# Attention: where a unit's output transposes stand, which engine inverts its sums, and one written order for each kind of two steps

## The chip, the cores and the metric

The kernel runs on one core of a Trainium2 chip. The metric is the device time in microseconds (us) of one execution; the time before is the median of three runs. The engines are TensorE (PE; its weight loads are shown apart as PEld), VectorE (DVE), ScalarE (ACT), GpSimd (POOL) and SyncE (SP, which only issues DMAs here).

## The reference, cut to what matters

One transformer block on 2048 rows of 576 columns, all in float32. The change lies in the attention.

```python
h = _layernorm(x) * (1 + ca) + sa
qkv = (h @ wqkv) -> q, k, v                     # 32 heads of 18 columns
scores = einsum("bhqd,bhkd->bhqk", q, k) * 18 ** -0.5
p = softmax(scores)                             # over 2048 keys
o = einsum("bhqk,bhkd->bhqd", p, v)
x = x + ga * (o.reshape(B, S, D) @ wo)
h = _layernorm(x) * (1 + cb) + sb
x = x + gb * ((sigmoid(h @ w_gate) * (h @ w_up)) @ w_down)
```

## The kernel before

The program has four stages: projections of q, k and v; the attention loop; the gated feed-forward part on the first 1024 rows; the same on the last 1024 rows. Only the attention loop is changed.

**Units, steps, periods.** A unit is two heads on one half of the query rows (1024 rows); there are 32 units (`u`), the number of pairs of heads (16) times two halves. A unit has 16 steps (`kt`), one for each 128 keys. The loop handles two steps at a time, an even one and the odd one after it; such two steps are called a period here, so a unit has eight periods, named by their even step: kt 0, 2, 4 to 14.

**What a step puts on PE.** Four score tiles (`t`, line 1055): 128 keys by 512 queries, for head h = 0 or 1 and column half c = 0 or 1; ACT turns each into exponentials (line 1059). Four maxima tiles (`m`, line 524): queries by 512 keys of a later unit, 22 steps ahead; DVE reduces each to row maxima (line 530). Of the eight maxima tiles of a period, one (head 0, keys 0, called `r` below) is copied by ACT with a Relu (line 533), and another (head 0, keys 1, called `x`) is joined with that copy by one DVE instruction (line 535). Head 0 lies in rows 0 to 63 of the PE array and head 1 in rows 64 to 127, so a tile of head 0 and one of head 1 that follow each other in the program run side by side: they are called a pair. Every tile takes the next of seven PSUM banks in turn (`bank()`), so a tile can be written only when the tile seven places before it has been read by ACT or DVE. The exponentials of a step are multiplied with v by `values()` (line 629): four column groups of the array at once, all 512 queries (`V`, `v` in the old strings) or 256 of them (the half runs `A` and `B`, `a` and `b`).

**Orders.** PE and ACT follow the order in which the code is written (a manual schedule); DVE, POOL and SP are ordered by the scheduler. The order of a step is a string, one letter for each action. Where a background step of TensorE is due (`state["next"] == "g"`), a period takes the order "full", otherwise "halved". In a halved period the even step runs the values of the step two before (`v`), then the first half of the last step's (`a`); the odd step runs the second half (`b`):

```python
order = ("vmmtmmtsactt", "wmcmbkttmtmt") if halved else ("vtmmttmvtm", "ktmwttmctmm")
```

The letters: `k` calls `taken()`, in which ACT copies the finished sums of a unit from PSUM to SBUF (`oT`, line 646). `w` or `s` starts what is due: at kt 3 `outputs()`, whose first part is four 128x128 transposes of `oT` into one bank (line 656); when a unit's maxima are complete `spread()`, one transpose (line 555); and one step of the background work (`rows0`, `rows1`: the projection with wo and the second layer norm of finished rows, whose PE parts are lines 743, 760, 776 and 886). `c` runs the second parts: for `outputs()` the reciprocal of the softmax sums on DVE, read from PSUM (line 661), ACT's copy of the bank (line 672), and two POOL multiplications into the rows of outputs (line 676). In the halved order `w` is the first thing of the odd step, so that the four transposes stand between a pair of score tiles and a pair of maxima tiles, after half run A and ahead of half run B. `SIDES`, `SIDES_H`, `MAXIMA` and `MAXIMA_H` say which head and column half each `t` and `m` takes.

**POOL's other work in the loop** is splitting and scaling `w_down` (units 4 to 14) and, from unit 15 on, the float32 splits of the background work that TensorE uses one or two periods later (lines 750, 751, 762 to 764, 866).

Of the kernel before, what the change touches and what calls it, by code (L numbers as in the profile page):

```python
# [15 lines left out]
F32 = mybir.dt.float32  # L16
F32R = mybir.dt.float32r
AF = mybir.ActivationFunctionType
ALU = mybir.AluOpType
# [4 lines left out]
P = 128  # L24
S = 2048
# [3 lines left out]
DH = 18  # L29
# [10 lines left out]
LEAD = 6  # L40
FROM0, FROM1 = 15 * 16, 27 * 16 + 8
# [6 lines left out]

MAXIMA = ((1, 0), (0, 0), (1, 1), (0, 2), (1, 2), (0, 3), (0, 1), (1, 3))
SINGLE = (0, 1)  # L50
MAXIMA_H = ((1, 0), (0, 0), (1, 1), (0, 2), (0, 3), (1, 2), (0, 1), (1, 3))
SIDES_H = ((1, 0), (1, 1), (0, 1), (0, 0))
SIDES = ((0, 0), (0, 1), (1, 0), (1, 1))
ORDERED = 7
SEVENS = NB - 2
TURNS = {1: 1, 6: 2, 2: 4, 7: 3, 5: 5, 4: 7, 3: 6}
ROWS_FROM = 1
SECOND = 7 * NB


@with_exitstack
def tile_block(ctx, tc, x_in, wqkv, wo, w_gate, w_up, w_down, c_in, w_mod, out):
    nc = tc.nc
# [10 lines left out]
    make_identity(nc, ident)  # L74
    powers = const.tile([P, 8], F32, name="powers")
    nc.gpsimd.memset(powers, -0.5)
    mcol = const.tile([P, 2, 5], F32, name="mcol")
    mcol2 = const.tile([P, 2, 6], F32, name="mcol2")
    gb_b = const.tile([P, D], F32, name="gb_b")
# [420 lines left out]
    def maxima():  # L500


        n = HW // P
        last = None
        for u in range(UNITS):
            qs, ks = heads(u)
            mx = mxs[u % 2]
            if u not in SINGLE and u - 2 in SINGLE:
                nc.gpsimd.memset(mx[:, 0:n, 1], LOWEST)
            for i in range(8 * n):  # L510
                if last is not None and i == (9 if u == 1 else 8):
                    if u == 1:
                        for _ in spread(*last):
                            pass
                    else:
                        state["spread"] = last
                qt = i // 8
                pairs = u not in SINGLE
                h, kc = (MAXIMA_H if state.get("halved") else MAXIMA)[i % 8]
                rows = slice(64 * h, 64 * h + 3 * DH)  # L520
                paired = pairs and h == 0 and kc < 2
                at = NCH if paired and kc == 0 else kc
                sp = bank()
                nc.tensor.matmul(  # L524
                    sp, qs[rows, qt * P : (qt + 1) * P],
                    ks[rows, at * 512 : (at + 1) * 512], start=True, stop=True,
                )
                to = mx[:, h * n + qt, kc : kc + 1]
                if not paired:
                    nc.vector.tensor_reduce(to, sp, axis=AX.X, op=ALU.max)  # L530
# [38 lines left out]
    todo = maxima()  # L569
    state = {}  # L570

    def turn():
        if turns["s"] < turns["to"]:
            turns["s"] += 1
            next(todo, None)

    def run():
# [71 lines left out]
    def outputs():  # L649
# [11 lines left out]
        nc.vector.reciprocal(rec, tq[:, :, :, DH])  # L661
        if half == 1 and p == H // 2 - 1:
            state["last"] = epool.tile([P, 512], F32, name="oT")[:, 0 : 16 * DH].rearrange("p (t e) -> p t e", t=8)
            for h in range(2):
                nc.vector.tensor_tensor(
                    state["last"][:, :, h * DH : (h + 1) * DH].rearrange("p (c b) e -> p c b e", c=2),
                    tq[:, 2 * h : 2 * h + 2, :, 0:DH],
                    rec[:, 2 * h : 2 * h + 2, :].unsqueeze(3).to_broadcast([P, 2, 4, DH]),
                    op=ALU.mult,
                )  # L670
            return
        nc.scalar.copy(oT, tp.rearrange("p b q -> p (b q)"))
        tq = oT.rearrange("p (b j e) -> p j b e", j=4, e=32)
        for h in range(2):
            f0 = (2 * p + h) * DH
            nc.gpsimd.tensor_tensor(
                Os[half][:, :, f0 : f0 + DH].rearrange("p (c b) e -> p c b e", c=2),
                tq[:, 2 * h : 2 * h + 2, :, 0:DH],
                rec[:, 2 * h : 2 * h + 2, :].unsqueeze(3).to_broadcast([P, 2, 4, DH]),
                op=ALU.mult,  # L680
            )
# [328 lines left out]
    for u in range(UNITS):  # L1010
# [5 lines left out]
            Os.append(big.tile([P, 8, 640], F32, name="big"))  # L1016
        for kt in range(NT):
            step = u * NT + kt
            turns["to"] = 64 + 4 * LEAD + 4 * (step + 1)
            kcols = slice(kt * P, (kt + 1) * P)  # L1020
            if kt % 2 == 0:
                heavy = state.get("next") == "g"
                hold = heavy and (kt == 2 or kt == 12 and u < UNITS - 1)
                state["halved"] = step >= 10 and (hold or not heavy)
            halved = state["halved"]
            sides = iter(SIDES_H if halved else SIDES)
            probs = [None] * 4
            order = ("vmmtmmtsactt", "wmcmbkttmtmt") if halved else ("vtmmttmvtm", "ktmwttmctmm")
            for does in order[kt % 2]:
                if does == "m":  # L1030
                    turn()
                elif does == "k":
                    taken()
                elif does in "ws":
                    if kt == 3:
                        follow.append(outputs())
                        next(follow[-1], None)
                    if "spread" in state and halved == (does == "s"):
                        follow.append(spread(*state.pop("spread")))
                        next(follow[-1])  # L1040
                    if step >= FROM0 and not hold and halved == (does == "s"):
                        state["next"] = next(rows0 if step < FROM1 else rows1, None)
                elif does == "c":
                    while follow:
                        next(follow.pop(0), None)
                elif does == "v":
                    if step >= LAG:
                        values()
                elif does in "ab":
                    values(slice(0, 256) if does == "a" else slice(256, 512))  # L1050
                else:
                    c, h = next(sides)
                    sT = bank()
                    rows = slice(64 * h, 64 * h + 3 * DH + 2)
                    nc.tensor.matmul(  # L1055
# [733 lines left out]
```

## Time and profile before

| | us |
|---|---|
| median of 3 runs | 2802.2 (2801.63 to 2802.61) |
| span of the profiled execution | 2801.3 |
| PE busy in it | 2766.6 (99%) |
| DVE busy | 2302.7 (82%) |
| ACT busy | 1607.0 (57%) |
| POOL busy | 816.2 (29%) |

The profiled execution is known by its span, from the first to the last instruction; the median of the runs is 0.9 us above it. Sums are made against the span and then shifted by these 0.9 us. The attention loop's values run from 238 us to 1534 us. PE's busy time counts modelled ends of overlapping matmuls; where PE loses time is therefore read from the starts of its rows in the timeline, not from its busy share.

### The profile page before, as it was taken

To read this page: it belongs to the slowest core of one execution; us is meant where nothing else is said; L and a number is where in the kernel's file an instruction comes from. 1 tells how busy PE (TensorE), PEld (TensorE's weight loads), DVE (VectorE), ACT (ScalarE), POOL (GpSimd) and SP (SyncE) were. 2 spreads that over 40 slices of the span, in tenths; PEclk is the share of its full clock that TensorE was granted. 3 is DMA by queue.
4 is the path that set the end of the run, shared out by engine and by line. 5 is a ranking of instruction groups with operands and counts; after the bars stand their busy time and mean duration, and the time that the engine had idled before them with its cause. 6 is when DMAs were issued, how large, how long until landed. Compare 5 with 4: busy or idle time off the path is not lost.

```text
span 2801.3 us, 50850 instructions
## 1 busy us (share of the span) xinstructions
PE 2766.6 (99%) x18637; PEld 1830.4 (65%) x18637; DVE 2302.7 (82%) x4370; ACT 1607.0 (57%) x3051; POOL 816.2 (29%) x1077
## 2 busy tenths in 40 slices
PE   7999999999999999999999999999999999999999
PEld 5975444444444444444444888888888888888888
DVE  7278999999998888999883788888898677777777
ACT  3216999999999778999888322333333222222221
POOL 3125208887843111663113222222221100000000
PEclk9999999999999999999999999999999999999999
DMA  5344215444442120232126766667767966666663
GB/s 173 123 155 147 72 59 173 168 173 157 170 135 80 36 59 24 98 106 71 43 68 219 266 220 228 232 217 266 279 249 274 355 201 196 203 196 200 199 197 120
DMA packets 170778, 462.60 MB, mean 165 GB/s; under 512 B 21212, under 2 KB 88032, under 8 KB 160416
## 3 DMA queue, kind: packets, MB, share of 16 engines
q1 hardware_dynamic: 150064, 360.72, 38.7%
q0 software_dynamic: 20464, 98.62, 10.0%
q8 instruction: 147, 2.41, 0.4%
q14 instruction: 103, 0.84, 0.1%
HBM read 281.92 MB, written 176.82 MB: 164 GB/s over the span
## 4 chain that ended last, share of the span: by engine, by line
PE 93%; DVE 4%; issue 1%; DMA 1%; ACT 1%; POOL 0%; SPq 0%; DVEq 0%; ACTq 0%; POOLq 0%
PE x L1196 28%; PE o L629 19%; PE s L1055 12%; PE s L524 10%; PE d L1346 8%; PE d L1278 6%; PE s L310 4%; PE s L776 2%; PE s L363 1%; DVE mx L530 1%; PE s L656 1%; ACT p L1059 1%; DMA wq_raw<-in_A_wqkv_dram 0%; DVE Oa L1350 0%; DVE w L1186 0%
## 5 line engine op out<-in xcount | busy, mean ns | idle before, releaser
L1059 ACT ACTIVATE p<-s 128x512 f32<-128x512 f32 x2048 | 1078.1, 621 | 98.8 <-PE s L1055 83.5
L530 DVE TENSOR_REDUCE mx<-s 128x1 f32<-128x512 f32 x1568 | 993.8, 683 | 108.0 <-PE s L524 93.3
L629 PE MATMUL o<-p,vaug 128*32 128x256 f32 (+1 forms) x5848 | 592.4, 477 | 3.1 <-ACT p L1059 2.5
L1055 PE MATMUL s<-q,k 56*128 56x512 f32 x1920 | 516.6, 449 | 0.0
L524 PE MATMUL s<-k,q 54*128 54x512 f32 x1920 | 501.3, 427 | 2.6 <-DVE t L746 1.7
L524 PEld LDWEIGHTS s<-k,q 54*128 54x128 f32 x1920 | 275.6, 185 | 231.6 <-DVE mx L535 161.0
L1055 PEld LDWEIGHTS s<-q,k 56*128 56x128 f32 x1920 | 246.9, 184 | 242.7 <-issue 112.8
L1196 PE MATMUL x<-k,w 128*128 128x512 f32 x1512 | 368.6, 391 | 0.0
L1196 PEld LDWEIGHTS x<-k,w 128*128 128x128 f32 x1512 | 276.9, 188 | 53.1 <-issue 1.7
L629 PEld LDWEIGHTS o<-p,vaug 128*32 128x32 f32 x5848 | 115.4, 108 | 209.7 <-issue 130.7
L1346 PE MATMUL d<-wd,hh 128*128 128x288 f32 x1248 | 249.9, 295 | 2.4 <-DVE Oa L1350 2.4
L1196 PE MATMUL x<-big,w 128*128 128x512 f32 x1008 | 244.9, 391 | 2.1 <-DVE u L1690 1.4
L1196 PE MATMUL x<-w,w 128*128 128x512 f32 x1008 | 245.1, 391 | 0.0
L1196 PEld LDWEIGHTS x<-big,w 128*128 128x128 f32 x1008 | 185.1, 188 | 38.5 <-DVE u L1690 2.3
L1196 PEld LDWEIGHTS x<-w,w 128*128 128x128 f32 x1008 | 184.4, 188 | 34.3
L1346 PEld LDWEIGHTS d<-wd,hh 128*128 128x128 f32 x1248 | 202.2, 188 | 6.2 <-DVE Oa L1350 3.1
L1346 PE MATMUL d<-wd,hl 128*128 128x288 f32 x624 | 184.3, 295 | 0.0
L1350 DVE TENSOR_TENSOR Oa<-Oa,d 128x288 f32<-128x288 f32 x312 | 136.4, 452 | 54.8 <-PE d L1346 50.8
L535 DVE CUSTOM_DVE_ANT_0 over<-s,over 128x512 f32<-128x512 f32 x240 | 164.4, 685 | 0.7 <-ACT p L1059 0.3
L533 ACT ACTIVATE over<-s 128x512 f32<-128x512 f32 x240 | 150.1, 626 | 7.4 <-PE s L524 7.3
L1205 ACT ACTIVATE sg<-x 128x512 f32<-128x512 f32 x36 | 21.6, 599 | 207.8 <-PE x L1196 207.8
L1177 ACT CAST w<-S 128x768 fp32r<-128x768 f32 x71 | 59.4, 836 | 137.5 <-POOL S L1150 135.6
(274 smaller groups left out, 3889.8 us busy)
## 6 DMA issues: line engine op xcount, KB each, us to landing
ws<-w SPq DMA_DIRECT2D x126, 640.0 KB
w<-ws SPq DMA_DIRECT2D x126, 640.0 KB
wd<-wds SPq DMA_DIRECT2D x19, 1152.0 KB
k<-kd SPq DMA_DIRECT2D x60, 360.0 KB
wds<-w POOLq DMA_DIRECT2D x18, 1152.0 KB, 5.6
wtd<-t POOLq DMA_DIRECT2D x32, 576.0 KB, 4.8
wt<-wtd SPq DMA_DIRECT2D x64, 288.0 KB
wd<-wds SPq DMA_DIRECT2D x52, 288.0 KB
```

Source lines behind the costliest of these rows:

```text
L310: nc.tensor.matmul(acc, w, hT[:, t, cols], start=n == 0, stop=n == len(ts_) - 1)
L524: nc.tensor.matmul(sp, qs[rows, qt * P : (qt + 1) * P], ks[rows, at * 512 : (at + 1) * 512], start=True, stop=True,)
L530: nc.vector.tensor_reduce(to, sp, axis=AX.X, op=ALU.max)
L533: nc.scalar.activation(over, sp, AF.Relu)
L535: nc.vector.tensor_tensor_reduce(out=over, in0=sp, in1=over, scale=1.0, scalar=LOWEST, op0=ALU.add, op1=ALU.max, accum_out=mx[:, h * n + q ...
L629: nc.tensor.matmul(acc[32 * j : 32 * j + 32, cols], vaug[:, kt, (2 * p + h) * VW : (2 * p + h) * VW + 32], probs[2 * c + h][:, cols], star ...
L1055: nc.tensor.matmul(sT, ks[rows, kcols], qs[rows, c * 512 : (c + 1) * 512], start=True, stop=True)
L1059: state["exp"] = nc.scalar.activation(pr, sT, AF.Exp, scale=SCALE)
L1196: nc.tensor.matmul(acc[v], w[:, v, a, :], X[s][:, b, :], start=first and n == 0, stop=n == 6, skip_group_check=not first,)
L1278: nc.tensor.matmul(acc, a[:, rows], w[:, k, :], start=n == 0, stop=n == 2)
L1346: nc.tensor.matmul(acc[:, :HALF], a[:, f, rows], w[:, f, cols], start=n == 0, stop=n == 5)
L1350: nc.vector.tensor_add(Oa[:, t, cols], Oa[:, t, cols], acc[:, :HALF])
```

## The change

Four things, all in the attention loop.

1. **The order of a period.** The two strings and the four tables of sides are replaced by a table `STEPS` with one text for both steps of a period: "full", "half", and own texts for the halved periods kt 0, 2, 4 and 12. Each word is a pair (`t0m1`: score tile of head 0 beside a maxima tile of head 1) or one action. `two_steps()` parses it once for each period: the first four score tiles belong to the even step, the column halves count up by head, and each maxima tile takes the next keys of its head (`r0` is keys 0 of head 0, `x0` keys 1). `turn()` passes head and keys to the maxima. As a period's order may now place its eight maxima freely over both steps, the allowance (`turns["to"]`) is raised by eight at the even step.
2. **Where the transposes stand.** `O` starts `outputs()` in the even step of kt 2, directly ahead of half run A. `S` starts `spread()` at kt 12 ahead of A, `G` the background step.
3. **The sums' inverses.** Except for the last unit, DVE's reciprocal is replaced by POOL: a copy of the sums from ACT's copy of the bank, a power of -1 with a constant tile, and two rounds of refinement with three operations each.
4. A constant tile `minus` is filled once on POOL.

```diff
+STEPS = {
+    "full": "V t0m1 r0t1 t0m1 V t1m0 K t0m1 G t1t0 m0 c t1 x0m1",
+    "half": "V t0m1 t0t1 m1m0 G A c r0m1 t1t0 B m1t0 x0t1 t1m0",
+    0: "V m1r0 t0t1 m0t1 G A c m1t0 m0m1 B K x0t1 t0t1 m1t0",
+    2: "V m1t0 t1t0 m0m1 O A c m1r0 t1m0 t1t0 G B c x0t1 m1t0",
+    4: "V r0m1 t1t0 m1m0 G A c t0t1 m1t0 B t1m0 m1t0 t1x0",
+    12: "V t0m1 m0t1 m1t0 S A c r0t1 m1t0 G B c t1t0 m1x0 t1m0",
+}
...
-    def turn():
+    def turn(*at):
         if turns["s"] < turns["to"]:
             turns["s"] += 1
+            state["at"] = at
             next(todo, None)
...
         rec = epool.tile([P, 4, 4], F32, name="rec")
-        nc.vector.reciprocal(rec, tq[:, :, :, DH])
         if half == 1 and p == H // 2 - 1:
+            nc.vector.reciprocal(rec, tq[:, :, :, DH])
...
         nc.scalar.copy(oT, tp.rearrange("p b q -> p (b q)"))
         tq = oT.rearrange("p (b j e) -> p j b e", j=4, e=32)
+        sums = epool.tile([P, 4, 4], F32, name="sums")
+        left = epool.tile([P, 4, 4], F32, name="left")
+        nc.gpsimd.tensor_copy(sums, tq[:, :, :, DH])
+        nc.gpsimd.tensor_tensor(rec, sums, minus.rearrange("p (j b) -> p j b", b=4), op=ALU.pow)
+        for _ in range(2):
+            nc.gpsimd.tensor_mul(left, sums, rec)
+            nc.gpsimd.tensor_scalar(left, left, -1.0, 2.0, op0=ALU.mult, op1=ALU.add)
+            nc.gpsimd.tensor_mul(rec, rec, left)
...
-            turns["to"] = 64 + 4 * LEAD + 4 * (step + 1)
+            turns["to"] = 64 + 4 * LEAD + 8 * (step // 2 + 1)
...
-            order = ("vmmtmmtsactt", "wmcmbkttmtmt") if halved else ("vtmmttmvtm", "ktmwttmctmm")
-            for does in order[kt % 2]:
+                order = two_steps(STEPS[kt if halved and kt in STEPS else "half" if halved else "full"])
+            for does, h, c in order[kt % 2]:
...
-                elif does in "ws":
-                    if kt == 3:
+                elif does in "OSG":
+                    if does == "O" or halved and kt == 2:
                         follow.append(outputs())
```

How the order of instructions moves is shown at two places. First PE, in a period kt 2 of an early unit: line 1055 (1088 after the change) are score tiles, 524 (551) maxima tiles, 629 (657) the values, 656 (684) the four transposes. Before:

```order
L1055 MATMUL s_7888<-q_1025,k_2233 128x512
L629 MATMUL o<-p_7859,vaug 32x256
L629 MATMUL o<-p_7841,vaug 32x256
L629 MATMUL o<-p_7852,vaug 32x256
L629 MATMUL o<-p_7845,vaug 32x256
L1055 MATMUL s_7896<-q_1025,k_2233 128x512
L1055 MATMUL s_7900<-q_1025,k_2233 128x512
L656 MATMUL s_7909<-ident,oT 128x128 x4
L524 MATMUL s_7914<-k_2236,q_1021 128x512
L524 MATMUL s_7922<-k_2236,q_1021 128x512
L629 MATMUL o<-p_7859,vaug 32x256
```

The same place of PE's program after the change:

```order
L551 MATMUL s_7960<-k_2238,q_1023 128x512
L551 MATMUL s_7963<-k_2238,q_1023 128x512
L684 MATMUL s_7966<-ident,oT 128x128 x4
L657 MATMUL o<-p_7922,vaug 32x256
L657 MATMUL o<-p_7933,vaug 32x256
L657 MATMUL o<-p_7918,vaug 32x256
L657 MATMUL o<-p_7926,vaug 32x256
L551 MATMUL s_7989<-k_2238,q_1023 128x512
L551 MATMUL s_7992<-k_2238,q_1023 128x512
L1088 MATMUL s_7996<-q_1027,k_2235 128x512
L551 MATMUL s_8005<-k_2238,q_1023 128x512
```

The four transposes have moved from between two single pairs to the place directly ahead of half run A; the pairs behind them stand together in longer runs. The second place is POOL's program in a later unit, at the projection of one tile of rows (756 is the copy whose transpose TensorE needs, 750, 751 and 762 belong to the split of the columns; 792, 786, 787 and 798 after the change). Before:

```order
L756 COPY t_13595<-Oa 128x128
L750 CAST t_13594<-t_13595 128x512
L751 TENSOR_TENSOR t_13594<-t_13595,t_13594 128x512
L676 TENSOR_TENSOR big<-oT,rec 128x8x18 x2
L762 CAST t_13594<-t_13595 64x128
```

The same place of POOL's program after the change:

```order
L792 COPY t_13795<-Oa 128x128
L704 COPY sums<-oT 128x16
L705 TENSOR_TENSOR rec<-sums,minus 128x16
L707 TENSOR_TENSOR left<-sums,rec 128x16
L708 TENSOR_SCALAR left<-left 128x16
L709 TENSOR_TENSOR rec<-rec,left 128x16
L707 TENSOR_TENSOR left<-sums,rec 128x16
L708 TENSOR_SCALAR left<-left 128x16
L709 TENSOR_TENSOR rec<-rec,left 128x16
L712 TENSOR_TENSOR big<-oT,rec 128x8x18 x2
L786 CAST t_13794<-t_13795 128x512
L787 TENSOR_TENSOR t_13794<-t_13795,t_13794 128x512
```

Eight small operations have come in ahead of the two multiplications, and the split that TensorE will use is now queued behind all ten; before the change it stood ahead of the two multiplications.

More of the change, by code (lines that the diff above doesn't have):

```diff
@@ L50 @@
 SINGLE = (0, 1)
-MAXIMA_H = ((1, 0), (0, 0), (1, 1), (0, 2), (0, 3), (1, 2), (0, 1), (1, 3))
-SIDES_H = ((1, 0), (1, 1), (0, 1), (0, 0))
-SIDES = ((0, 0), (0, 1), (1, 0), (1, 1))
+STEPS = {
[6 rows of a table added]
+}
 ORDERED = 7
@@ L58, with two_steps @@
 SECOND = 7 * NB
+def two_steps(text):
+    steps, scores = ([], []), 0
+    keys = {"r0": [0], "x0": [1], "m0": [2, 3], "m1": [0, 1, 2, 3]}
+    for word in text.split():
+        for does in (word[:2], word[2:]):
+            if not does:
+                continue
+            if scores % 4 == 0:
+                sides = {"t0": [0, 1], "t1": [0, 1]}
+            to = steps[scores >= 4]
+            if does in sides:
+                to.append(("t", int(does[1]), sides[does].pop(0)))
+                scores += 1
+            elif does in keys:
+                to.append(("m", int(does[1]), keys[does].pop(0)))
+            else:
+                to.append((does, None, None))
+    return steps
 @with_exitstack
@@ L76, in tile_block @@
     nc.gpsimd.memset(powers, -0.5)
+    minus = const.tile([P, 16], F32, name="minus")
+    nc.gpsimd.memset(minus, -1.0)
     mcol = const.tile([P, 2, 5], F32, name="mcol")
@@ L518, in maxima @@
                 pairs = u not in SINGLE
-                h, kc = (MAXIMA_H if state.get("halved") else MAXIMA)[i % 8]
+                h, kc = state.get("at") or MAXIMA[i % 8]
                 rows = slice(64 * h, 64 * h + 3 * DH)
@@ L1023, in tile_block @@
                 hold = heavy and (kt == 2 or kt == 12 and u < UNITS - 1)
-                state["halved"] = step >= 10 and (hold or not heavy)
-            halved = state["halved"]
-            sides = iter(SIDES_H if halved else SIDES)
+                halved = step >= 10 and (hold or not heavy)
+                order = two_steps(STEPS[kt if halved and kt in STEPS else "half" if halved else "full"])
             probs = [None] * 4
-            order = ("vmmtmmtsactt", "wmcmbkttmtmt") if halved else ("vtmmttmvtm", "ktmwttmctmm")
-            for does in order[kt % 2]:
+            for does, h, c in order[kt % 2]:
                 if does == "m":
-                    turn()
-                elif does == "k":
+                    turn(h, c)
+                elif does == "K":
                     taken()
-                elif does in "ws":
-                    if kt == 3:
+                elif does in "OSG":
+                    if does == "O" or halved and kt == 2:
                         follow.append(outputs())
                         next(follow[-1], None)
-                    if "spread" in state and halved == (does == "s"):
+                    if "spread" in state:
                         follow.append(spread(*state.pop("spread")))
                         next(follow[-1])
-                    if step >= FROM0 and not hold and halved == (does == "s"):
+                    if does == "G" and step >= FROM0 and not hold:
                         state["next"] = next(rows0 if step < FROM1 else rows1, None)
@@ L1045, in tile_block @@
                         next(follow.pop(0), None)
-                elif does == "v":
+                elif does == "V":
                     if step >= LAG:
                         values()
-                elif does in "ab":
-                    values(slice(0, 256) if does == "a" else slice(256, 512))
+                elif does in "AB":
+                    values(slice(0, 256) if does == "A" else slice(256, 512))
                 else:
-                    c, h = next(sides)
                     sT = bank()
```

## Prediction

> **What bounds the kernel now.** I read the page first: the busy line, the granted clock and the chain that ended last.
>
> ```profile
> span 2801.3 us, 50850 instructions
> PE 2766.6 (99%) x18637; PEld 1830.4 (65%) x18637; DVE 2302.7 (82%) x4370; ACT 1607.0 (57%) x3051; POOL 816.2 (29%) x1077
> PE 93%; DVE 4%; issue 1%; DMA 1%; ACT 1%; POOL 0%; SPq 0%; DVEq 0%; ACTq 0%; POOLq 0%
> ...
> L530 DVE TENSOR_REDUCE mx<-s 128x1 f32<-128x512 f32 x1568 | 993.8, 683 | 108.0 <-PE s L524 93.3
> L1055 PEld LDWEIGHTS s<-q,k 56*128 56x128 f32 x1920 | 246.9, 184 | 242.7 <-issue 112.8
> ```
>
> PE is on the chain for 93%. The change touches the attention loop alone, and there the busy times of the stretch from 445 to 1000 us say which engine is next (columns: length, then PE, PEld, DVE, ACT, POOL with counts, clock, DMA share, GB/s):
>
> ```profile
> 445.00:1000.00 555.00, 554.48 (x4582) 236.97 (x4583) 502.74 (x962) 517.07 (x1039) 335.07 (x534) 1.00 0.39 134
> ```
>
> The clock is 1.00 throughout. PE has no gap that its busy time shows; ACT is busy for 93%, DVE for 91%. PE's rows overlap, so I read what it loses from the distance between starts, in the timeline of PE over a period kt 2 and the next one (start, length, line, operation):
>
> ```profile
> 702.64 1.07 PE L629 MATMUL o<-p,vaug 128*32 128x512 f32 x8
> 703.63 0.73 PE L524 MATMUL s<-k,q 54*128 54x512 f32 x3
> 703.98 0.39 PE L1055 MATMUL s<-q,k 56*128 56x512 f32 x1
> 704.21 0.40 PE L524 MATMUL s<-k,q 54*128 54x512 f32 x1
> ...
> 704.61 0.64 PE L629 MATMUL o<-p,vaug 128*32 128x256 f32 x8
> 705.18 0.50 PE L1055 MATMUL s<-q,k 56*128 56x512 f32 x2
> 705.61 0.66 PE L656 MATMUL s<-ident,oT 128*128 128x128 f32 x4
> 706.20 0.49 PE L524 MATMUL s<-k,q 54*128 54x512 f32 x2
> 706.62 0.64 PE L629 MATMUL o<-p,vaug 128*32 128x256 f32 x8
> 707.19 0.73 PE L1055 MATMUL s<-q,k 56*128 56x512 f32 x3
> 707.53 0.39 PE L524 MATMUL s<-k,q 54*128 54x512 f32 x1
> 707.76 0.40 PE L1055 MATMUL s<-q,k 56*128 56x512 f32 x1
> ...
> 708.09 1.07 PE L629 MATMUL o<-p,vaug 128*32 128x512 f32 x8
> ...
> 710.56 0.50 PE L1055 MATMUL s<-q,k 56*128 56x512 f32 x2
> 710.90 0.43 PE L524 MATMUL s<-k,q 54*128 54x512 f32 x2
> 711.25 0.64 PE L629 MATMUL o<-p,vaug 128*32 128x256 f32 x8
> ...
> 712.73 1.07 PE L629 MATMUL o<-p,vaug 128*32 128x512 f32 x8
> ```
>
> The two tiles of a pair start together, so each pair is one step of this list. The prices are the differences. A run of three pairs costs 0.34 + 0.23 + 0.33 = 0.90 (707.19, 707.53, 707.76, 708.09); a run of two 0.34 + 0.33 = 0.67, the last step taken from the run before (710.56 to 711.25 shows 0.69); a single pair 0.43 (705.18) or 0.42 (706.20). So the first pair of a run costs 0.43 and every further one 0.23 or 0.24: a change between kinds of matmul costs about 0.2. V takes 0.99, a half run 0.57.
>
> **The transposes' new place.** Before, a period kt 2 has its eight pairs in runs of 3, 1, 1 and 3, with the transposes between the single ones: 0.90 + 0.43 + 0.42 + 0.90 = 2.65, and 0.59 from the transposes to the next pair (705.61 to 706.20). After, `STEPS[2]` has runs of 3, 3 and 2: 0.90 + 0.90 + 0.67 = 2.47. The transposes stand directly ahead of A; what that costs is shown by the four equal transposes of line 743, which already stand there:
>
> ```profile
> 868.34 0.65 PE L743 MATMUL s<-ident,Oa 128*128 128x128 f32 x4
> 868.92 0.64 PE L629 MATMUL o<-p,vaug 128*32 128x256 f32 x8
> ```
>
> 0.58 instead of 0.59. A period kt 2 gets 0.18 + 0.01 = 0.19 shorter. It happens 31 times:
>
> ```profile
> L672 ACT COPY oT<-s x31: 586/736/747, 281.6 to 1503.7; 128x512 f32<-128x512 f32 x31
> L661 DVE RECIPROCAL rec<-s x32: 199/257/258, 281.2 to 1537.4; 128x16 f32<-128x16 f32 x32
> ```
>
> 31 x 0.19 = **-6.0 us**, and nothing else has to become faster for it, since PE itself is the chain. A second effect lies at the same place: A started 0.40 after the last pair (704.21 to 704.61) where an unhindered one takes 0.33. A waits for the last exponential of the step before, late because ACT has copied the unit's sums in between. Now 0.58 of transposes stand ahead of A and cover these 0.07: 31 x 0.07 = **-2.2 us**. What could be late next is the transposes themselves, which need that copy; it is queued ahead of the exponentials that A waits for, so it is done first.
>
> **The other orders.** Starts of V in one unit (698 to 736 us; 702.64, 708.09 and 712.73 stand above), with the one transpose of `spread`:
>
> ```profile
> 697.93 1.06 PE L629 MATMUL o<-p,vaug 128*32 128x512 f32 x8
> ...
> 717.42 1.07 PE L629 MATMUL o<-p,vaug 128*32 128x512 f32 x8
> ...
> 722.12 1.07 PE L629 MATMUL o<-p,vaug 128*32 128x512 f32 x8
> ...
> 726.81 1.07 PE L629 MATMUL o<-p,vaug 128*32 128x512 f32 x8
> ...
> 728.70 0.28 PE L555 MATMUL s<-ident,nm 128*16 128x128 f32 x1
> ...
> 731.74 1.06 PE L629 MATMUL o<-p,vaug 128*32 128x512 f32 x8
> ...
> 736.36 1.07 PE L629 MATMUL o<-p,vaug 128*32 128x512 f32 x8
> ```
>
> The periods kt 0 to 14 last 4.71, 5.45, 4.64, 4.69, 4.70, 4.69, 4.93 and 4.62. With runs of 3, 2 and 3 the least is 0.99 + 0.90 + 0.57 + 0.67 + 0.57 + 0.90 = 4.60. Beyond it lie 0.11, 0.04, 0.09, 0.10, 0.09 and 0.02, and at kt 12 some 0.1 besides the transpose's 0.2 to 0.28: about 0.55 a unit outside kt 2, or 31 x 0.55 = 17 us in all, if the later units were like this one. The new orders keep runs of 3, 2 and 3 (3, 3, 2 at kt 2), so these waits are all that they can change: at best -17. At worst they add as much again, +17, since ACT has nine tiles a period at 517.07 / 1039 = 0.50, 4.5 of 4.69, and DVE seven at 993.8 / 1568 = 0.63, 4.4: with seven banks in turn, an order can only push a wait to another pair. I take kt 4 and kt 12 to lose 0.03 and 0.05, and kt 0 to gain 0.10: there the seventh tile, a maxima tile, starts DVE anew only after A (start 0.99 + 0.90 + 0.57 = 2.47 after V, 0.50 for the tile, 0.68 for its reduction), the ninth follows 0.63 later, at 4.28, and the last pair, due at 4.27 behind a weight load, reuses that bank. Net +0.02 a unit, **+0.5 us**, nearest to no change because ACT's nine and DVE's seven tiles are the same as before. "full" keeps PE's order letter for letter: 0.
>
> **The end of the loop.** From unit 30, kt 10 on no maxima are left, and the new texts then put two score tiles of one head next to each other: one more single slot, 0.23, in each of the seven halved periods left, up to 1.6. But ACT sets the pace there (a row of the period at 1523.11, with PE's idle time):
>
> ```profile
> 1525.14 0.64 PE L629 MATMUL o<-p,vaug 128*32 128x256 f32 x8 [0.53 <-ACT p L1059]
> ```
>
> I take **+0.3**.
>
> **The inverses on POOL.** DVE loses 31 x 0.257 = 8 us of work, worth nothing by itself: DVE is not the chain, and the bank was held for ACT's copy anyway. POOL gets eight operations. No row has a power of 16 elements; the layer norms' give 4 and 8:
>
> ```profile
> L197 POOL TENSOR_TENSOR r<-var,powers 128x4 f32<-128x4 f32 x6 | 6.6, 1106 | 44.9 <-DVE var L196 44.9
> L197 POOL TENSOR_TENSOR r<-var,powers 128x8 f32<-128x8 f32 x1 | 1.7, 1679 | 19.8 <-DVE var L196 19.8
> ...
> L763 POOL CAST t<-t 64x128 fp32r<-64x128 f32 x8 | 2.3, 293 | 0.5
> ```
>
> 0.143 for each further element: 1.68 + 8 x 0.143 = 2.8, and seven small operations at no more than the 0.29 of a 128-wide cast: 2.0. Some 4.8 a unit, 150 us of an engine with 1985 us free. Its queue is in order, so `w_down`'s splits and the splits of the background rows stand behind it. The tightest place is the last split of a projected tile, then TensorE's use of it in the next full period:
>
> ```profile
> 957.71 0.46 POOL L764 TENSOR_TENSOR t<-t,t 64x128 fp32r<-64x128 f32 x1
> 961.75 0.43 PEld L776 LDWEIGHTS s<-w,t 128*128 128x128 f32 x3 [0.37 <-issue]
> ```
>
> Ended at 958.17, used at 961.75: 3.6 of slack against 4.8, but the outputs now start 1.1 us earlier in their period (702.64 + 0.99 + 0.90 instead of 705.61), so the delay about fits. **0**, between 0 and +4 (four tiles at most with 1 us each). `minus` is filled once while PE waits for the first loads; the scheduler also moves one q load behind three others of its unit on SP, which are read ten steps (some 23 us) later: 0. POOL only multiplies once ACT's copy is there, as before.
>
> **Sum.** -6.0 - 2.2 + 0.5 + 0.3 = -7.4 on a span of 2801.3; the median of the runs is 0.9 above the span: 2801.3 - 7.4 + 0.9 = **2794.8 us**.
>
> [...] Where two tiles of the same head are neighbours across a pair's border, the rows show no price: 703.98 to 704.21 is 0.23 with different heads at the border, 707.53 to 707.76 is 0.23 with the same head. [...]
>
> **Rivals.**
> - *The orders remove the waits too.* kt 0 and 12 have the longest waits, and each has its own text. Against: the ordinary periods' 0.09 are an ACT queue that is full. If 0.35 of the 0.55 a unit goes, another 11 us: 2783.
> - *The time comes back as waits.* PE runs 0.26 a unit earlier against an ACT that is 93% busy, or POOL's delay reaches TensorE by a few us. Against: ACT has 38 us idle in those 555. If half or more comes back, and POOL costs 2: 2799 to 2803.
> - *Slower: one pair of the ordinary periods waits.* In the new "half" the third pair behind V is two maxima tiles, and the banks that it takes held score tiles of the step before; if their exponentials are half a job (0.25) later than now, that is 102 x 0.25 = 25.5, or 2820. It decides from 13 / 102 = 0.13 a period on. For it: the queue of ACT is as tight as this. Against: V's 0.99 lies between.
>
> **How the numbers follow.** The forecast has 0.53 (2791 to 2798, of it 0.50 below the bound that follows), the removed waits 0.13, the time that comes back 0.28, the slower order 0.05, the rule 0.01. About 0.2%, 5.6 us, is what a measurement of this kernel can tell from no change: faster means below 2796.6. So faster 0.63, no difference 0.31, slower 0.06. The range 2787 to 2802 leaves out most of the removed waits' case, the slower ones and the upper end of the third.
>
> **What would show it.** The period kt 2 should last 5.2 instead of 5.45, with runs of 3, 3 and 2 pairs and a start of A right 0.58 after the transposes. kt 0 should be some 0.1 longer. The power should take about 2.8 us, POOL's busy time rise by some 130 to 150, and no row of line 776 or 886 (their new numbers) wait for POOL. Wrong I would be if the ordinary periods moved by more than 0.05 either way, or if the transposes themselves waited for a bank.

## The result, and the profile after

The change made the kernel slower: 2834.6 us (median of 4 runs, 2832.4 to 2837.5) against 2802.4 before (2801.6 to 2807.0). The ratio is 1.0107, with a 95% interval of 1.0093 to 1.0121. The forecast was 2794.8. Medians and ratios leave out two slow executions of the variants further below, at a mean granted clock of 0.61 and 0.56 (3939.8 and 4314.7 us). The profiled run took 2837.5 with a span of 2835.7, 34.4 more than before. Its page:

```profile
span 2835.7 us, 50718 instructions
...
PE 2793.9 (99%) x18637; PEld 1855.4 (65%) x18637; DVE 2310.1 (81%) x4339; ACT 1611.6 (57%) x3051; POOL 952.8 (34%) x1326
...
PE 85%; POOL 6%; DVE 4%; DMA 3%; issue 2%; ACT 0%; SPq 0%; DVEq 0%; ACTq 0%; POOLq 0%
...
L1229 PE MATMUL x<-k,w 128*128 128x512 f32 x1512 | 376.2, 395 | 0.0
L1229 PE MATMUL x<-big,w 128*128 128x512 f32 x1008 | 251.3, 398 | 2.5 <-DVE u L1723 2.3
```

The same groups before:

```profile
L1196 PE MATMUL x<-k,w 128*128 128x512 f32 x1512 | 368.6, 391 | 0.0
L1196 PE MATMUL x<-big,w 128*128 128x512 f32 x1008 | 244.9, 391 | 2.1 <-DVE u L1690 1.4
```

Two things stand out. POOL and DMA, which were on 1% of the chain, are now on 9%. And the feed-forward matmuls, which the diff does not touch, take 395 to 398 ns where they took 391, without any wait. The stretches of both programs say where the 34.4 us lie: from the first to the last matmul of the values 1310.3 against 1296.3 us, ahead of it 0.7, behind it 1286.2 against 1266.6. So 14.7 us were lost by the end of the attention and 19.6 in a stage that nobody edited.

**The two pauses.** In the attention I took the start of the values at each unit's first period and its difference to before (table further below). It jumps twice, by 7 us near 785 and by 8 near 886. What waited there (engine, line, for whom: us in total, times, longest):

```profile
PEld o L657 <- ACT oT L674: 5.5, 1, 5.5
ACT oT L674 <- POOL Oa L712: 5.3, 1, 5.3
PE o L657 <- ACT oT L674: 5.2, 1, 5.2
...
PEld s L796 <- POOL t L792: 4.6, 1, 4.6
PE s L796 <- POOL t L792: 4.1, 1, 4.1
```

The values wait for ACT's copy in `taken()`, and that copy waits for POOL's multiplication of the unit before, which still reads the one `oT` buffer. POOL's timeline ahead of the first pause (start, length):

```profile
777.32 0.73 POOL L950 DMA_DIRECT2D w<-in_B_w_down_dram  x1 [0.91 <-DMA wds<-w]
778.04 0.21 POOL L704 COPY sums<-oT 128x16 f32<-128x16 f32 x1
778.21 0.81 POOL L998 TENSOR_TENSOR t<-t 128x288 fp32r<-128x288 f32 x1
778.98 2.94 POOL L705 TENSOR_TENSOR rec<-sums,minus 128x16 f32<-128x16 f32 x1
781.88 0.60 POOL L999 DMA_DIRECT2D wtd<-t  x1
782.51 0.23 POOL L707 TENSOR_TENSOR left<-sums,rec 128x16 f32<-128x16 f32 x1
...
784.32 0.81 POOL L712 TENSOR_TENSOR Oa<-oT,rec 128x144 f32<-128x144 f32 x2
```

This chain belongs to transposes that TensorE made at 744.25: POOL begins it 34 us later, almost a unit (38 us). From the ends of line 712 and the starts of line 674 (676 and 646 before) I worked out how much room is left between a multiplication and the next copy into `oT`: in units 1 to 4 it is 27.6 to 29.3 us (32.0 to 32.8 before), in units 5, 6, 7, 9, 10 and 13 then 21.4, 14.7, 7.1, 4.1, 0.0 and 0.0 (27.4, 23.3, 24.9, 23.6, 28.8 and 21.3 before). That is the time of `w_down`'s splits: the chain is a few us a unit too much for a queue that is nearly full, and the arrears pile up from unit 5 to unit 13. The second pause does not come from the `oT` buffer but from the order of the queue: on POOL, line 792 stands directly behind the chain of output 16 (880.59 to 886.50), and the transpose needs it at 882.7 (two lines of POOL, then one of PE):

```profile
885.69 0.81 POOL L712 TENSOR_TENSOR Oa<-oT,rec 128x144 f32<-128x144 f32 x2
886.57 0.29 POOL L792 COPY t<-Oa 128x128 f32<-128x128 f32 x1
...
886.91 0.48 PE L796 MATMUL s<-ident,t 128*128 128x128 f32 x1 [4.15 <-POOL t L792]
```

**The clock.** The two pauses cost 7.1 and 8.2 us, more than the 5.19 and 4.25 for which PE is idle in the windows at 780 and 880 (columns: window, length, PE, PEld, DVE, ACT, POOL busy with counts, granted clock, DMA share, GB/s):

```profile
241.00:242.00 1.00, 1.00 (x8) 0.83 (x6) 0.07 (x1) 0.10 (x1) 0.71 (x1) 0.50 1.12 233
780.00:790.00 10.00, 4.81 (x22) 2.01 (x20) 3.21 (x8) 3.96 (x8) 9.47 (x19) 0.71 0.69 237
790.00:800.00 10.00, 10.00 (x86) 4.06 (x88) 8.13 (x16) 8.94 (x19) 9.52 (x16) 0.95 0.19 78
880.00:890.00 10.00, 5.75 (x39) 1.92 (x37) 4.99 (x10) 3.61 (x7) 8.93 (x18) 0.83 0.26 90
890.00:900.00 10.00, 10.00 (x68) 4.50 (x60) 6.28 (x13) 6.54 (x14) 0.00 (x0) 0.83 0.00 0
```

Read in windows of 1 us, the clock from 100 us on falls to 0.50 at 238 to 244, 784 to 790, 886 to 893, 1094 to 1098 and 1569 to 1572. Each stretch loses 1.7 or 3.4 us of full speed; in the attention they sum to 11.9. Before, there was none between 28 and 2803 us.

**What the change gained.** A period kt 2 with its transposes, the forecast's main place:

```profile
665.51 1.07 PE L657 MATMUL o<-p,vaug 128*32 128x512 f32 x8
666.51 0.49 PE L551 MATMUL s<-k,q 54*128 54x512 f32 x1
666.51 0.73 PE L1088 MATMUL s<-q,k 56*128 56x512 f32 x3
667.09 0.40 PE L551 MATMUL s<-k,q 54*128 54x512 f32 x2
667.41 0.66 PE L684 MATMUL s<-ident,oT 128*128 128x128 f32 x4
668.00 0.64 PE L657 MATMUL o<-p,vaug 128*32 128x256 f32 x8
...
669.47 0.64 PE L657 MATMUL o<-p,vaug 128*32 128x256 f32 x8
...
670.71 0.64 PE L657 MATMUL o<-p,vaug 128*32 128x512 f32 x4
```

This is 5.20 from V to V, and 0.59 from the transposes to A. The medians of the halved periods without other work, from the starts of V, for four kernels (the third and fourth are experiments below):

| period | before | changed | reciprocal on DVE, new place | reciprocal on DVE, late |
|---|---|---|---|---|
| kt 0 | 4.71 | 4.80 | 4.81 | 4.81 |
| kt 2 | 5.45 | 5.19 | 5.72 | 5.31 |
| kt 4, 6, 8, 10 | 4.64, 4.69, 4.69, 4.69 | 4.63, 4.66, 4.63, 4.66 | 4.63, 4.66, 4.63, 4.66 | 4.63, 4.66, 4.63, 4.67 |
| kt 12, 14 | 4.93, 4.62 | 4.96, 4.60 | 4.97, 4.60 | 4.97, 4.59 |

By these medians a plain unit, one without other work, is 0.29 us shorter in the changed kernel than before.

### The profile page after: what moved, and what is told of

It is laid out like the page before. It is cut to its first block, busy times and chain, and to the rows that moved or that the text cites. A ratio compares the mean times of both kernels' runs of the same rounds, so it can differ in the third digit from the quotient of the medians.

```text
span 2835.7 us, 50718 instructions
## 1 busy us (share of the span) xinstructions
PE 2793.9 (99%) x18637; PEld 1855.4 (65%) x18637; DVE 2310.1 (81%) x4339; ACT 1611.6 (57%) x3051; POOL 952.8 (34%) x1326
## 4 chain that ended last, share of the span: by engine, by line
PE 85%; POOL 6%; DVE 4%; DMA 3%; issue 2%; ACT 0%; SPq 0%; DVEq 0%; ACTq 0%; POOLq 0%
PE x L1229 28%; PE o L657 15%; PE s L1088 9%; PE s L551 9%; PE d L1379 8%; PE d L1311 6%; PE s L337 4%; PE s L812 2%; PE s L390 1%; DMA wds<-w 1%; POOL w L968 1%; DVE mx L557 1%; DMA wtd<-t 1%; POOL rec L705 1%; POOL w L971 1%
## 5 line engine op out<-in xcount | busy, mean ns | idle before, releaser
L1092 ACT ACTIVATE p<-s 128x512 f32<-128x512 f32 x2048 | 1061.3, 613 | 87.1 <-PE s L1088 52.0
L557 DVE TENSOR_REDUCE mx<-s 128x1 f32<-128x512 f32 x1568 | 1006.3, 685 | 113.1 <-PE s L551 69.0
L657 PE MATMUL o<-p,vaug 128*32 128x256 f32 (+1 forms) x5848 | 598.6, 481 | 5.7 <-ACT oT L674 5.6
L551 PE MATMUL s<-k,q 54*128 54x512 f32 x1920 | 580.1, 443 | 1.9 <-DVE t L782 1.1
L1088 PE MATMUL s<-q,k 56*128 56x512 f32 x1920 | 539.2, 434 | 1.3 <-DVE mx L557 1.1
L551 PEld LDWEIGHTS s<-k,q 54*128 54x128 f32 x1920 | 272.2, 185 | 233.4 <-DVE mx L557 69.4
L1088 PEld LDWEIGHTS s<-q,k 56*128 56x128 f32 x1920 | 253.8, 185 | 230.3 <-ACT p L1092 118.8
L1229 PE MATMUL x<-k,w 128*128 128x512 f32 x1512 | 376.2, 395 | 0.0
L1229 PE MATMUL x<-big,w 128*128 128x512 f32 x1008 | 251.3, 398 | 2.5 <-DVE u L1723 2.3
L560 ACT ACTIVATE over<-s 128x512 f32<-128x512 f32 x240 | 143.6, 598 | 22.4 <-PE s L551 18.6
```

What stands on the lines that cost most here:

```text
L551: nc.tensor.matmul(sp, qs[rows, qt * P : (qt + 1) * P], ks[rows, at * 512 : (at + 1) * 512], start=True, stop=True,)
L657: nc.tensor.matmul(acc[32 * j : 32 * j + 32, cols], vaug[:, kt, (2 * p + h) * VW : (2 * p + h) * VW + 32], probs[2 * c + h][:, cols], star ...
L1088: nc.tensor.matmul(sT, ks[rows, kcols], qs[rows, c * 512 : (c + 1) * 512], start=True, stop=True)
L1092: state["exp"] = nc.scalar.activation(pr, sT, AF.Exp, scale=SCALE)
L1229: nc.tensor.matmul(acc[v], w[:, v, a, :], X[s][:, b, :], start=first and n == 0, stop=n == 6, skip_group_check=not first,)
```

## The experiments

Each ratio is to the kernel before, executed beside it. "Pace" is the mean distance between the starts of neighbouring 128x512 matmuls of the feed-forward stage, worked out from the trace (3528 matmuls, distances up to 300 ns): 228.3 ns before, 233.4 after. The expectations put it at 229 and 234, since they counted distances up to 400. 3528 x 5.07 ns = 17.9 us, and with the halved clock at 1569 to 1572 (1.7) that is the stage's 19.6.

**1. The constant tile alone, in the kernel before.**

```diff
+    minus = const.tile([P, 16], F32, name="minus")
+    nc.gpsimd.memset(minus, -1.0)
```

> The kernel before with nothing added but the changed kernel's constant tile of 16 columns (64 bytes a partition, filled once and never read), which moves every tile allocated after it on that side by 64 bytes, the feed-forward stage's weight tiles among them. Theory A (place): the feed-forward matmuls of 128x512 start 233.9 ns apart instead of 228.8, as in the changed kernel, 3528 times 5.1 ns = 18 us, so about 2820 us. Rival B (the slower matmuls come from something that the changed attention leaves behind, such as the clock): 2802 us and 229 ns.

2822.0 us, ratio 1.0061 (1.0045 to 1.0076), pace 233.4 ns, attention 1296.7. Theory A holds: a tile that nobody reads costs 18 us, by where it puts the tiles behind it.

**2. The changed kernel, with the tile taken elsewhere.**

```diff
-    minus = const.tile([P, 16], F32, name="minus")
+    minus = epool.tile([P, 16], F32, name="minus")
```

> The changed kernel with the constant tile taken from the attention's own small pool, so that no tile of the feed-forward stage lies elsewhere than before. Theory A: the feed-forward matmuls are back at 229 ns, and the time is 2834.6 - 18 = about 2816 us, with the two pauses of TensorE of 4 to 5 us behind GpSimd's chain (and the halved clock after them) still there. Rival B: 2834 us and 234 ns.

2817.2 us, ratio 1.0048 (1.0034 to 1.0063), pace 228.3; pauses of 5.27 at 785 and of 2.93 and 2.31 at 880 and 888. This is as expected.

**3. The reciprocal back on DVE, at the new place.**

```diff
+        nc.vector.reciprocal(rec, tq[:, :, :, DH])
         if half == 1 and p == H // 2 - 1:
-            nc.vector.reciprocal(rec, tq[:, :, :, DH])
...
-        sums = epool.tile([P, 4, 4], F32, name="sums")
...
-            nc.gpsimd.tensor_mul(rec, rec, left)
```

> The changed kernel's orders and its earlier transposes, but the sums inverted by VectorE from PSUM as before; no chain on GpSimd and none of its three tiles. Theory C (GpSimd's queue makes the attention's loss): no pause over 4 us, period 2 at 5.2 us, and 2802.4 - 6.0 (two switches fewer in period 2) + 0.8 (the other periods) and 0 to 2 us for the reciprocal = 2797 to 2799 us. Rival D (the earlier transposes or the orders make the pauses themselves, the chain only stands in them): pauses at the same places and 2805 us or more.

2814.6 us, ratio 1.0035 (1.0022 to 1.0048). No pause over 1.2 us in the attention, as theory C said, but no gain either: C missed the time, and D the pauses. Period 2 takes 5.72 us. Waits in one of them:

```profile
ACT oT L698 <- DVE rec L687: 0.5, 1, 0.5
PEld s L549 <- ACT oT L698: 0.4, 1, 0.4
```

ACT's copy of the bank waits for DVE's reciprocal, which is queued behind DVE's reductions. Over the 31 outputs these waits come to 14.6 us, where they were 0.7 before; the kernel before stands first:

```profile
L672 ACT COPY oT<-s 128x512 f32<-128x512 f32 x31 | 21.1, 680 | 0.7 <-DVE rec L661 0.7
...
L698 ACT COPY oT<-s 128x512 f32<-128x512 f32 x31 | 18.2, 589 | 14.6 <-DVE rec L687 14.6
```

So the inverse had to leave this place for the earlier transposes to pay: 5.72 against 5.19.

**4. Only the chain on POOL, in the orders of before.** `minus` in `epool`, as in 2; `outputs()` with the changed kernel's nine lines on POOL, at the old place.

> The kernel before, its orders and the place of its transposes, with only the inversion moved to GpSimd (constant tile in the attention's small pool, so the feed-forward stage lies as before). Theory C: the copy that takes an output waits for GpSimd near 780 us and the projected rows wait near 885 us, 9 us of pauses and some 5 us of halved clock: 2812 to 2818 us. Rival D: no such pauses, 2799 to 2803 us.

2816.2 us, ratio 1.0042 (1.0028 to 1.0055). Pauses of 1.56 at 783, 1.07 at 876 and 2.62 at 883. Theory C holds: the chain makes pauses at both places in the old orders too. The first is shorter than the 5.19 us of the changed kernel, so the new orders have a share in that one; how they get it is not shown. Kt 2 stays at 5.46, so by itself the chain gains nothing.

The differences to before at the start of a unit's values (us, from the traces) put runs 2 to 5 and 8 side by side:

| after units | changed | 2 | 3 | 4 | 5 | 8 |
|---|---|---|---|---|---|---|
| 0 | +0.8 | +1.5 | +0.1 | +0.8 | +0.9 | +0.4 |
| 1 | +3.4 | +2.8 | +2.8 | +2.2 | +3.7 | +0.5 |
| 13 | +1.2 | +0.2 | +5.6 | +2.2 | +2.9 | -2.0 |
| 15 | +8.3 | +6.8 | +6.0 | +3.8 | +2.6 | -2.6 |
| 17 | +16.2 | +15.6 | +6.8 | +12.7 | +2.6 | 0.0 |
| 20 | +16.6 | +15.9 | +8.4 | +12.7 | +2.9 | +0.2 |
| 21 | +18.4 | +19.1 | +10.7 | +12.9 | +4.8 | +3.4 |
| 31 | +16.4 | +17.1 | +12.9 | +12.8 | +3.1 | +0.7 |
| 32 (end) | +14.7 | +15.4 | +11.2 | +12.8 | +1.4 | -0.9 |

The first jump is a halved clock, those between 13 and 17 units are the pauses. At the last, at 21, DVE waits for a layer norm's power on POOL, before (first line) and after:

```profile
DVE sd L200 <- POOL r L197: 1.3, 1, 1.3
...
DVE sd L227 <- POOL r L224: 1.8, 1, 1.8
```

The kernel before and its nine versions with shifted tiles all wait 1.3 us here; PE pauses for 0.91 to 0.94 us, and the clock stays full. The eight kernels with a changed attention wait 1.5 to 2.1 us; PE pauses for 1.13 to 1.43, and in six of the eight half clock follows. The power itself takes as long as before (1.64 to 1.68 us); why the wait grew is not shown.

**5. The reciprocal on DVE, but later.**

```diff
         nc.scalar.copy(oT, tp.rearrange("p b q -> p (b q)"))
+        yield "again"
         tq = oT.rearrange("p (b j e) -> p j b e", j=4, e=32)
...
+        nc.vector.reciprocal(rec, tq[:, :, :, DH])
```

The chain's nine lines on POOL go. `yield "again"` leaves the rest to the next `c`, behind half run B.

> The changed kernel's orders and its earlier transposes; VectorE inverts the sums again, but from ACT's copy in SBUF and behind the second half run of values of that period instead of between the two; nothing on GpSimd but the multiplications, no added tile. If the place of the reciprocal in VectorE's order is what made period 2 take 5.72 us in the run with VectorE's reciprocal at the new place: period 2 at 5.2 us, 31 ordinary and other units 0.26 us shorter each, so 2804 - 8 = 2795 to 2798 us, and no pauses behind GpSimd. If 16 columns more on VectorE cost their time wherever they stand: period 2 at 5.45 us or more, 2803 to 2812 us.

2802.5 us beside 2806.4 before, ratio 0.9984 (0.9974 to 0.9993). Period 2 takes 5.31, between the two expectations, and there is no pause behind POOL. This version is faster than the kernel before by 0.16%, about 4 us, half of the 8 that I expected. Why period 2 does not come down to 5.2 is not shown.

**6, 7, 9, 10, 13, 15, 16. What about the place?** All are the kernel before with a tile that nobody uses: 64 bytes in front of the weight tiles `w0` to `w2`, with `w3` and `w4` left in place (6); a constant tile of 8, 32, 24 or 64 columns (7, 9, 10, 13); 64 bytes in front of `opool` on the other side, which moves the moving tiles down (15); 48 columns and that (16). The edit of run 7, without the line that fills the tile:

```diff
+    minus = const.tile([P, 8], F32, name="minus")
```

> The kernel before with 64 bytes put in front of a part of the feed-forward tiles only: the weight tiles w0, w1 and w2 (and the two gate tiles and the sums of weights) move by 64 bytes, w3 and w4 and all else stay. If the place of a matmul's own weights sets its pace: the matmuls with w0 to w2 start 234 ns apart, those with w3 and w4 229 ns. If it is another tile or something common to all: one pace for all five, 229 or 234 ns.

> The kernel before with a constant tile of 8 columns, a shift of 32 bytes instead of 64. If only whole steps of 64 bytes are harmless or harmful by their parity (the weights lie at 96 modulo 128 before, at 32 after a shift by 64): here they lie at 0 modulo 128, and the pace is 229 ns or less, 2802 us; if every shift from the place of before costs the same: 234 ns and 2820 us.

> The kernel before with a constant tile of 32 columns: a shift by 128 bytes, after which the feed-forward weights lie at 96 modulo 128 again. If the pace goes by the place modulo 128: 228 ns between the feed-forward matmuls, as before, about 2804 us. If it goes by a larger step, or any shift hurts: 233 ns and 2821 us.

> The kernel before with a constant tile of 24 columns: a shift by 96 bytes, the feed-forward weights at 64 modulo 128. If only the place of before (96, which is where the moving tiles lie too) is fast: 233 ns, 2821 us. If the two upper places 64 and 96 are alike, as 0 and 32 were: 228 ns.

> The kernel before with a constant tile of 64 columns: a shift by 256 bytes, after which the feed-forward weights lie at the same place modulo 512 as the moving tiles (480). If the pace goes by the place modulo 256 or smaller steps: 228 ns, about 2804 us. If 256 matters too: 232 to 234 ns, 2817 to 2823 us.

> The kernel before with 64 bytes put in front of the tiles of the other side, from which the feed-forward matmuls take the moving rows: these lie 64 bytes lower, the weights stay. If the place of the weights alone sets the pace: 228 ns. If the distance between the two does: 232 to 234 ns, 2817 to 2823 us, as after a shift of the weights.

> The kernel before with the feed-forward weights 192 bytes higher and the moving tiles 64 bytes lower: both now lie at 160 modulo 256, where both lay at 224 before. If the distance between weights and moving rows modulo 256 sets the pace: 228 ns, about 2804 us. If it is the place of each: 232 to 234 ns, 2817 to 2823 us.

| run | weights' shift | moving tiles' shift | distance changed by, modulo 256 | pace, ns | one run, us |
|---|---|---|---|---|---|
| before | 0 | 0 | 0 | 228.3 | 2802.4 (median) |
| 7 | +32 | 0 | 32 | 233.4 | 2823.0 |
| 1 | +64 | 0 | 64 | 233.4 | 2822.0 (median) |
| 10 | +96 | 0 | 96 | 234.2 | 2822.1 |
| 9 | +128 | 0 | 128 | 232.2 | 2815.0 |
| 13 | +256 | 0 | 0 | 228.3 | 2806.8 |
| 15 | 0 | -64 | 64 | 233.4 | 2819.0 |
| 16 | +192 | -64 | 0 | 228.3 | 2803.9 |

In run 6 (2815.8 us), with the matmuls told apart by their place in the program, those with `w0`, `w1` and `w2` go at 233.3 to 233.4 ns, `w3` at 229.3, `w4` at 228.2: each matmul follows its own weights. Before, by the addresses that the program gives its tiles, weights and moving rows lie at the same place modulo 256 (224). At the distances tried, the pace goes by the distance modulo 256, not by the place of either: runs 13 and 16 move one or both and stay fast, while 1 and 15 move one each and are slow. All but before and run 1 were executed once, and each pace comes from one trace. My first guesses, a parity of 64 bytes (7) and a period of 128 (9), fell. One window of each shows it in the profile, by the matmuls in 100 us (the x behind PE's busy time); runs 1, 13, 15 and 16:

```profile
2300.00:2400.00 100.00, 100.00 (x537) 86.72 (x536) 77.74 (x156) 23.39 (x39) 0.00 (x0) 1.00 0.60 195
```

```profile
2300.00:2400.00 100.00, 100.00 (x543) 87.75 (x542) 78.70 (x159) 23.02 (x39) 0.00 (x0) 1.00 0.61 198
```

```profile
2300.00:2400.00 100.00, 100.00 (x537) 86.71 (x536) 78.02 (x157) 23.40 (x39) 0.00 (x0) 1.00 0.62 199
```

```profile
2300.00:2400.00 100.00, 100.00 (x543) 87.75 (x542) 78.72 (x159) 23.41 (x39) 0.00 (x0) 1.00 0.61 201
```

537 or 543 with the clock at 1.00 and PE busy throughout.

**8. A shorter chain.** Run 2 without the refinement.

```diff
-        for _ in range(2):
-            nc.gpsimd.tensor_mul(left, sums, rec)
-            nc.gpsimd.tensor_scalar(left, left, -1.0, 2.0, op0=ALU.mult, op1=ALU.add)
-            nc.gpsimd.tensor_mul(rec, rec, left)
```

> The changed kernel with its constant tile in the attention's small pool (feed-forward tiles as before) and without the two refinements of the inverse (6 of the 9 small operations on GpSimd left out, 1.8 of 5.2 us for each output, so the quotients are less exact). If it is the sum of the chains over units 5 to 13 that makes GpSimd late (it started to multiply 38 us after the copy at output 13, with 5 us of that the chain itself): 9 x 1.8 = 16 us less lateness, no pause near 785 us (5.2 us and 3.4 us of clock saved), the one near 886 us 1.8 us shorter: 2817 - 10 = 2807 us. If the pauses come from GpSimd's waits for its transfers and not from the length of the chain: both pauses stay, 2815 us or more.

2804.8 us, ratio 0.9991 (0.9982 to 1.0). The pause at 785 is gone, the other is 2.38 at 873.5:

```profile
780.00:790.00 10.00, 10.00 (x92) 4.32 (x84) 9.00 (x18) 9.91 (x20) 9.66 (x16) 1.00 0.51 186
```

The room behind output 13 is 2.3 us, where it was 0.0. So it is the sum of the chains over the full units that decides, as the first expectation said. Against the kernel before, this version is not clear of no difference.

**11. Period 0 in the common order.**

```diff
-    0: "V m1r0 t0t1 m0t1 G A c m1t0 m0m1 B K x0t1 t0t1 m1t0",
+    0: "V t0m1 t0t1 m1m0 G A c r0m1 t1t0 B K m1t0 x0t1 t1m0",
```

> The run with the late reciprocal on VectorE, but period 0 in the common order of the halved periods (with the taking of the output where the kernel before has it, behind the second half run) instead of its own. If its own order is what makes period 0 take 4.80 us (4.71 before): 4.70 us, 31 times 0.1 = 3 us less, ratio to before about 0.997. If period 0 needs its own order for what follows in period 2: period 2 rises from 5.31 us by what period 0 wins, ratio 0.998 to 1.0.

2811.0 us, ratio 1.0023 (1.0012 to 1.0033); period 0 takes 5.13 us instead of 4.81. Neither expectation: the next V waits for the copy of the unit's sums.

```profile
PE o L655 <- ACT oT L672: 0.4, 1, 0.4
```

Period 0's own order avoids this wait among the new orders. It costs 0.09 against the kernel before; no run shows an order that gives that back.

**12. The chain only where POOL has time.** As 11, with the chain for outputs 1 to 4 and 17 to 31, and 5's late reciprocal for the others.

```diff
+        if 5 <= half * (H // 2) + p + 1 <= 16:
+            yield "again"
+            nc.vector.reciprocal(rec, tq[:, :, :, DH])
+        else:
...
```

> As the run with the plain period 0, but GpSimd inverts the sums of outputs 1 to 4 and 17 to 31, where it started to multiply 5 us (at most 17 us) behind the copy in the changed kernel, and VectorE late those of outputs 5 to 16, where GpSimd was up to 38 us late (constant tile in the attention's small pool). If the backlog of units 5 to 16 alone made the pauses: none over 1.5 us behind the chain, period 2 at 5.19 us in 19 units instead of 5.31, 2 us less than the run with the plain period 0, ratio about 0.996 to 0.997. If the chain costs elsewhere too: no less than that run.

2811.3 us, ratio 1.0033 (1.0022 to 1.0045). There is no pause behind the chain at either place, as expected; but nothing is gained on run 11 (1.0023) that the ratios could tell, so half of the expectation failed. The traces show how little there was to gain: in the plain units where the chain stands (1, 3, 23, 24 and 26 to 30) period 2 takes 5.19 to 5.21, as expected, but beside run 11's 5.28 to 5.31 that is only about 0.09 a unit, in nine units instead of 19, under 1 us in all.

**17. The same rule in the attention?** 224 bytes in front of the queries.

```diff
+    qpad = left.enter_context(tc.tile_pool(name="qpad", bufs=1))
+    nc.gpsimd.memset(qpad.tile([P, 56], F32, name="pad"), -1.0)
```

> The kernel before with 224 bytes put in front of the query tiles, so that queries and keys lie at the same place modulo 256 in the attention's score matmuls (they lie 32 apart before); the feed-forward tiles stay. If the same rule holds for these matmuls of 56 and 54 rows that run in pairs, and they set the attention's pace: the pairs start closer than 232 ns and the attention of 1296 us gets shorter, by up to 2 % (26 us). If their pace is not set by this: 1296 us from the first to the last matmul of values, as under every other shift.

2805.8 us in one run; the attention takes 1299.1, of which 3.4 us go to a halved clock at 238 to 244, so 1296 as always. The pairs' pace is not set by it.

## Why the prediction was wrong

*The switches at kt 2, -6.0, and A's wait, -2.2:* right, where the unit is plain (31 x 0.19 is 5.9; I had written 6.0). Kt 2 took 5.19 where 5.26 was to follow from the first term and 5.2 from both, with runs of 3, 3 and 2 and A 0.59 behind the transposes. The other units gave less; in units 2 and 4, for one, kt 2 rose from 6.08 to 6.24. Outside the jumps in the table the changed kernel gained 5.8 us in all, not 7.4.

*Kt 0 (+0.10), kt 4 (-0.03), kt 12 (-0.05) and the ordinary periods (0):* they moved by +0.09, -0.01, +0.03, and -0.02 to -0.06. Kt 0 was right, kt 12 went the other way, and kt 8 with -0.06 is just past the 0.05 that I had allowed. In sum this is -0.03 a unit where I took +0.02. The rivals that moved these periods did not come: neither the removed waits nor the late bank, whose factor of 102 counts the halved periods outside kt 0, 2, 4 and 12. No run shows a term for "the rule" with its chance of 0.01; what they show of the ordinary periods is the -0.02 to -0.06. The loop's end was put at +0.3; the last unit gained 1.7 instead.

*"worth nothing by itself: DVE is not the chain, and the bank was held for ACT's copy anyway":* wrong at the new place of the transposes. Run 3 shows 0.53 us at kt 2 for DVE's reciprocal, since the copy itself waits behind DVE; at the old place, in run 4, its move gained nothing. I had credited the gain to the switches alone; it needed the inverse's move as well.

*The chain on POOL, 0, "between 0 and +4":* the step that failed first. Its prices were right: 2.93 us for the power (2.8), 5.2 from the first copy to the multiplication (4.8), and 136.6 us more of busy time (130 to 150).

```profile
L705 POOL TENSOR_TENSOR rec<-sums,minus 128x16 f32<-128x16 f32 x31 | 90.8, 2929 | 2.2
```

The cover was wrong. I set 150 us against 1985 us of free time, an average over stages, and looked for the tightest place among single steps of the projected rows. What decides is a queue that was 76 to 84% busy in each 100 us from 500 to 800 before the change, and a backlog that is carried from unit to unit. The rows of lines 812 and 922 that I named waited for POOL only a little (1.3 and 3.2 us in all); the long waits came at 674 and 796. The rival in which "POOL's delay reaches TensorE by a few us" had the mechanism, with 2 us for it; with the half clock that followed the pauses it cost 15.3 (7.1 and 8.2).

*"`minus` is filled once while PE waits for the first loads":* the other failed step, and the larger. I costed the fill and not the place that the tile takes, which moves every tile behind it. Run 1 measures that at 18 us.

*The clock:* no step had it. Besides the pauses' share, 2.6 us were lost at 238, where a run of either kernel may lose them or not (12 of 18 profiles did), and 1.8 at 1093, which goes with the change: six of the eight changed attentions had half clock there, none of the ten others.

The sum of after against before, with the gain, the pauses, the later start, and the clock at 238 and 1093: -5.8 + 15.3 + 0.8 + 2.6 + 1.8 = 14.7 by the end of the attention. Behind it, the tile's place and the clock at 1569: 17.9 + 1.7 = 19.6.

## What to carry to other kernels

Count an added tile as a change to everything that is allocated behind it, and look at the addresses of matmul operands in stages that you did not touch; if an untouched group's mean changes without any wait, test the tile alone. For work that goes to another queue, compare it with that queue's free time in the busiest stage, and add up what is left over from unit to unit until the buffer that it holds is needed again. And a move that pays may pay only together with its companion: try each half.

## What the runs showed of the hardware

In these runs a 128x512 matmul of the feed-forward stage whose stationary and moving tiles lie at the same place modulo 256 bytes (224 or 160) followed its neighbour after 228.3 ns; at distances of 32, 64, 96 and 128 it took 233.4, 233.4, 234.2 and 232.2. Why is not shown. The two places count together: with one of them moved by 64 bytes the pace was 233.4 (runs 1 and 15), with both moved, by 192 and -64, it was 228.3 (run 16).

The 1872 matmuls of 128x288 in the larger of their two groups kept their mean (132.8 to 133.0 in all runs), but no run could have moved it: one half of them lies at distance 0 and the other at 128 in every one, as their two tiles move together or not at all. Told apart by the addresses in the program (distances in time up to 200 ns), neighbours at distance 0 follow each other after 131.3 ns in the kernel before and those at 128 after 133.4 (131.4 to 132.1 and 133.0 to 134.2 in the changed kernel and runs 7, 10 and 15), so these matmuls depend on the distance too. The attention's length did not follow the shifts.

The granted clock fell to half for 3.41 us at a time, for two of these, or, in run 2 at 881, for three. In the traces of before and after, every stretch between two of its changes is a whole multiple of 3.4133 us: after, 1 or 2 of these at half clock, and at full clock between the dips from 245 us on 539.31, 95.57, 201.39 and 471.04, which are 158, 28, 59 and 138 of them. Why is not shown. Pauses of 1.13 to 1.43 us near 1085 were followed by half clock in 6 of 8 profiles, of 0.91 to 0.94 at that place in none of 10, but the pause of 0.93 to 0.95 at the attention's start in 12 of 18: in these profiles the length of a pause alone does not tell. The same pause cost nothing, 1.7 or 3.4 us. That fits a part of the spread between runs of one kernel: the kernel before took 2801.5 to 2809.1 us at a mean granted clock of 0.999 or 1.000, and 2807.2 to 2811.7 at 0.996 or 0.997.
